# Grouped-query decode attention with a gated FFN on one core: K and V blocks alternate, and eight row blocks of wo go between the last two V blocks

## The chip, the cores and the metric

The kernel runs on one core of one Trainium2 chip. The metric is the device time of one execution in microseconds (us); lower is better. Three runs of the kernel before took 357.87 (median), 356.19 and 358.83 us.

## The reference

One token is decoded. The result is a gated mix of an attention branch with a cached K and V of 32768 positions and of a small SwiGLU branch. All inputs are bf16.

```python
# x 1x1x512, wq 512x4096, k_cache and v_cache 1x8x32768x128, wo 4096x512
# w_gate, w_up 512x1792, w_down 1792x512, gate_w 512
g = sigmoid((x * gate_w).sum(-1, keepdims=True))
q = (x @ wq) as 32 heads of 128                      # 4 query heads per K/V head
p = softmax(q . k * 128 ** -0.5)                     # over 32768 positions
a = (p . v, as one row of 4096) @ wo
b = (silu(x @ w_gate) * (x @ w_up)) @ w_down
out = g * a + (1 - g) * b
```

K and V are 134.2 of the 148.1 MB that are read. With one query position, each of these bytes is used once.

## The kernel before

**Blocks and pages.** There are G = 8 groups (K/V heads). K and V of a group are each cut into NB = 2 blocks of 16384 positions, 4.19 MB or 32 KB per partition. SBUF holds five pages of that size. K's two blocks use pages 0 and 2 (`PG_K`), V's two blocks pages 1 and 3 (`PG_V`). Page 3 holds w_gate and w_up first (`PG_F`), and page 4 (`PG_X`) holds wq first and wo at the end.

**Loads.** All of these loads are issued by SyncE (SP), strictly in the order of its program, onto one queue. Each issue may first wait. `load_k(g, b)` (L278) waits until TensorE has transposed all of block b of K of the group before (`sem_fill`), since that frees the page. `load_v(g, b)` (L283) waits until TensorE has finished with block b of V of the group before (`sem_v_free`); for group 0 the second V block waits until w_gate and w_up are used (`sem_pe_h`). The order is: wq, w_gate, w_up, both K blocks of group 0, the first V block of group 0, both K blocks of group 1, the second V block of group 0; then, for each further group g, both K blocks of g and both V blocks of g - 1; then both V blocks of group 7, w_down (`wd`), and wo in five pieces.

**TensorE.** A loop (L508) makes nine passes, i = 0, 16, ..., 128. In pass g it does `emit_k` (L403) for both blocks of group g, and then `emit_v` (L429) for both V blocks of group g - 1. The first pass skips the V part, the last one skips the K part and ends with `emit_end`. The parts are skipped with `pe.If` on the loop's register.

- `emit_k(i, b)` waits for the page and works in 8 units. For each unit, `emit_fill` makes 8 transposes (L382, two bf16 positions at a time as fp32) into PSUM, VectorE copies the result to SBUF (`ktT`, L663), and `emit_scores` (L394) makes 16 matmuls with q; the scores run two units behind the transposes. VectorE then takes the maximum over the block (L668).
- The maximum over all positions of a group needs both of its K blocks. GpSimd reduces it over the partitions (`gmax`, L266), and ScalarE writes the exponentials of both blocks into `ET` (L541); it waits until the V block of the group before has used that half of `ET` (`sem_v_free`).
- `emit_v(i, b)` waits for the V page and for the exponentials and makes 32 matmuls of 512 columns into `ps_o` (L438). Ahead of the first block, `emit_reduce` (L416) gathers what the group before has left in `acc` (8 matmul records, L420). ScalarE copies `ps_o` to `acc` (L553) when both V blocks are done.

**The end.** `emit_end` (L471) sums the exponentials, reduces the last group, multiplies `wd` (14 matmuls of 512 columns, `emit_wide`, L450, rotating over four strips of PSUM partitions into `ps_w`), brings the attention output into the order of wo's rows (`O2`), and goes through wo's 32 row blocks. The first piece (20 blocks) uses `emit_wide`; VectorE copies `ps_w` to `part` (L699). Each later block uses `emit_rows` (4 matmuls of 128 columns, L461), and `part` is added with the same helper. Then the row is cast (L701) and stored.

Of the kernel before, what the change touches and what calls it, by code (L numbers as in the profile page):

```python
# [13 lines left out]
def bass_gated_mix__gqa_block_cached__swiglu_ffn__decode_kernel(  # L14
# [14 lines left out]
    G = A_k_cache.shape[1]  # L29
# [13 lines left out]
    NB = S // BLK  # L43
# [10 lines left out]
    STEP = 16  # L54
    WOJ = H * DH // 128
    SCALE = float(DH) ** -0.5
    assert UPG == STEP and UPP % NKT == 0 and UPP % NST == 0
    assert KC * H * DH <= PAGE and 2 * KC * F <= PAGE and WOJ * NOUT <= PAGE
    WO_CUTS = [0, 20, 26, 29, 31, 32]
    OC = NOUT // 128  # L60

    RQ = 4
# [1 line left out]
    NSTRIP = 4  # L64
# [8 lines left out]
    with ExitStack() as es:  # L73
        def S_(name):
            return es.enter_context(nc.semaphore(name))
# [3 lines left out]
        sem_f = S_("s_f")  # L79
        sem_wo = [S_(f"s_wo{i}") for i in range(len(WO_CUTS) - 1)]  # L80
        sem_ld_x = S_("s_ld_x")
# [13 lines left out]
        sem_pe_q = S_("s_pe_q")  # L95
# [31 lines left out]
        def T(name, shape, dt):  # L127
            return es.enter_context(nc.sbuf_tensor(name, shape, dt))
# [44 lines left out]
        O2 = T("O2", [128, WOJ], BF16)  # L173
# [27 lines left out]
        wo_v = page[:, PG_X, 0 : WOJ * NOUT].rearrange("p (j n) -> p j n", j=WOJ)  # L201

        with nc.Block("main") as block:
# [66 lines left out]
            @block.sync  # L270
            def _(sp):
                def cache(which, g, b, p, sem):
                    sp.dma_start(  # L273
                        page[:, p, :].rearrange("p (r d) -> p r d", d=DH),
                        which[0, g, b * BLK : (b + 1) * BLK, :].rearrange("(p r) d -> p r d", r=R),
                    ).then_inc(sem, 16)

                def load_k(g, b):  # L278
                    if g:
                        sp.wait_ge(sem_fill, UPG * (g - 1) + UPP * (b + 1))  # L280
                    cache(A_k_cache, g, b, PG_K[b], sem_page[PG_K[b]])

                def load_v(g, b):  # L283
                    if g:
                        sp.wait_ge(sem_v_free, NB * (g - 1) + b + 1)
                    elif PG_V[b] == PG_F:
                        sp.wait_ge(sem_pe_h, 1)
                    cache(A_v_cache, g, b, PG_V[b], sem_page[PG_V[b]])

                sp.dma_start(wq_v, A_wq.rearrange("(p c) n -> p c n", c=KC)).then_inc(sem_q, 16)  # L290
                for w, src in enumerate((B_w_gate, B_w_up)):
                    sp.dma_start(  # L292
                        wgu[:, w, :, :], src.rearrange("(p c) f -> p c f", c=KC)
                    ).then_inc(sem_f, 16)
                for b in range(NB):
                    load_k(0, b)
                load_v(0, 0)
                for b in range(NB):
                    load_k(1, b)
                load_v(0, 1)  # L300
                for g in range(2, G):
                    for b in range(NB):
                        load_k(g, b)
                    for b in range(NB):
                        load_v(g - 1, b)
                for b in range(NB):
                    load_v(G - 1, b)
                sp.dma_start(  # L308
                    wd[:, :, :], B_w_down.rearrange("(p j) n -> p j n", j=FC)
                ).then_inc(sem_ld_wd, 16)  # L310
                sp.wait_ge(sem_pe_q, 1)
                src = A_wo.rearrange("(p j) n -> p j n", j=WOJ)
                for k, s in enumerate(sem_wo):
                    a, b = WO_CUTS[k], WO_CUTS[k + 1]
                    sp.dma_start(wo_v[:, a:b, :], src[:, a:b, :]).then_inc(s, 16)
                sp.wait_ge(sem_dve_row, 1)
                sp.dma_start(
                    out[0, 0, :].rearrange("(c n) -> c n", c=OC),
                    res_row[0 : 32 * (OC - 1) + 1 : 32, :],
                ).then_inc(sem_out, 16)  # L320
                sp.wait_ge(sem_out, 16)

            @block.tensor
            def _(pe):
                pe.wait_ge(sem_ld_x, 32)
                pe.wait_ge(sem_const, 1)
                for src, base in ((x_row, M_X0), (gw_row, M_X0 + KC)):
                    srcv = src[0:1, :].rearrange("o (p c) -> o c p", c=KC)
                    for c in range(KC):
                        ins = pe.matmul(  # L330
                            ps_m[:, base + c : base + c + 1],
                            srcv[:, c, :],
                            ones_bf[0:1, 0:1],
                            start=True,
                            stop=True,
                        )
# [4 lines left out]
                for h in range(H):  # L341
                    for c in range(KC):
                        ins = pe.matmul(  # L343
                            ps_m[:, M_Q0 + h : M_Q0 + h + 1],
                            wq_v[:, c, h * DH : (h + 1) * DH],
                            xT[:, c : c + 1],
                            start=(c == 0),
                            stop=(c == KC - 1),
                        )
# [3 lines left out]
                for e in range(2):  # L353
                    ins = pe.matmul(
                        ps_o[:, e * H : (e + 1) * H],
                        perm[:, e, :],
                        qT[:, :],
                        start=True,
                        stop=True,
                    )  # L360
# [3 lines left out]
                for w, base in enumerate((M_G0, M_U0)):  # L364
                    for j in range(FC):
                        for c in range(KC):
                            ins = pe.matmul(  # L367
                                ps_m[:, base + j : base + j + 1],
                                wgu[:, w, c, :].rearrange("d (p j) -> d j p", j=FC)[:, j, :],
                                xT[:, c : c + 1],  # L370
                                start=(c == 0),
                                stop=(c == KC - 1),
                            )
# [74 lines left out]
                def emit_wide(w, vec, j, first, last):  # L448
                    c = j % NSTRIP
                    return pe.matmul(  # L450
                        ps_w[32 * c : 32 * c + 1, :],
                        vec[:, j : j + 1],
                        w[:, j, :],
                        start=first,
                        stop=last,
                        skip_group_check=True,
                    )
# [13 lines left out]
                def emit_end():  # L471
                    pe.wait_ge(sem_dve_esum2, 1)
                    pe.matmul(  # L473
                        ps_e[:, 0:H],
                        ones_f[:, :],
                        esum2[:, :, :].rearrange("p g h -> p (g h)"),
                        start=True,
                        stop=True,
                    ).then_inc(sem_pe_S, 1)
                    emit_reduce((G + 1) * STEP)  # L480
                    pe.wait_ge(sem_dve_tT, 1)
                    pe.wait_ge(sem_ld_wd, 16)
                    pe.wait_ge(sem_psw, 1)
                    for j in range(FC):
                        emit_wide(wd, tT, j, j < NSTRIP, False)
                    pe.wait_ge(sem_dve_oT2, 1)
                    pe.wait_ge(sem_dve_pm, 1)
                    pe.matmul(
                        ps_m[:, M_O0 : M_O0 + WOJ], pmat[:, :], O2a[:, :], start=True, stop=True
                    ).then_inc(sem_pe_O2, 1)  # L490
                    pe.wait_ge(sem_dve_O2, 1)
                    for k, s in enumerate(sem_wo):
                        pe.wait_ge(s, 16)
                        for j in range(WO_CUTS[k], WO_CUTS[k + 1]):
                            if k == 0:
                                ins = emit_wide(wo_v, O2, j, False, j >= WO_CUTS[1] - NSTRIP)
                            else:
                                ins = emit_rows(
                                    O2[:, j : j + 1], wo_v[:, j, :], j == WO_CUTS[1], j == WOJ - 1
                                )  # L500
                        if k == 0:
                            ins.then_inc(sem_pe_w, 1)
                        if k == 1:
                            pe.wait_ge(sem_dve_w, 1)
                            emit_rows(sel4[:, 0:1], part[:, :], False, False)
                    ins.then_inc(sem_pe_sum, 1)

                with pe.Fori(0, (G + 1) * STEP, STEP) as i:  # L508
                    with pe.If(i < G * STEP):
                        for b in range(NB):  # L510
                            emit_k(i, b)
                    with pe.If(i > 0):
                        for b in range(NB):
                            emit_v(i, b)
                    with pe.If(i > (G - 1) * STEP):
                        emit_end()
# [213 lines left out]
```

## Time and profile before

| | |
|---|---|
| median of three runs | 357.87 us |
| profiled execution: time, span | 358.76 us, 357.0 us |
| granted TensorE clock, mean | 0.871 |
| read from HBM, mean rate over the span | 148.11 MB, 415 GB/s |
| DMA queue of the loads, share of 16 engines | 97.1% |
| TensorE matmuls, weight loads, VectorE, ScalarE busy | 71%, 61%, 50%, 9% |
| chain that ended last: DMA, TensorE, VectorE | 61%, 35%, 3% |
| a K load, a V load, issue to landing (median) | 26.2 us, 30.9 us |
| five wo loads, issue to landing | 28.9, 30.3, 30.7, 31.0, 30.8 us |

The span is the profiled execution as the trace has it. The chain that ended last is followed back from the last instruction, at each step to what released it; its shares tell which kind of work the end waited for, where busy shares don't.

### The profile page before, as it was taken

Reading aid. Unit: us, or ns where it says so; the run is one execution under the profiler, and the core shown is the slowest. Engines: PE = TensorE matmul, PEld = TensorE weight load, DVE = VectorE, ACT = ScalarE, POOL = GpSimd, SP = SyncE. Lnnn points to the kernel's source line nnn. Section 1 sums busy time; section 2 is a strip of 40 time slices with the busy share of each in tenths; the row PEclk is TensorE's granted clock in tenths of the full one; section 3 lists DMA queues with packets and bytes.
Section 4 is the critical chain, followed back from the end, with each engine's and each line's share of the span. In section 5 each row is a group of like instructions: output and inputs, shape, how many; then the busy total and the mean of one; then the engine's idle time right before and its main releaser. Section 6 shows DMA issues by size and latency. Waiting matters only on the chain.

```text
span 357.0 us, 8699 instructions
## 1 busy us (share of the span) xinstructions
PE 252.9 (71%) x3999; PEld 218.6 (61%) x3999; DVE 177.8 (50%) x203; ACT 33.5 (9%) x148; POOL 5.8 (2%) x24
## 2 busy tenths in 40 slices
PE   0346984989989639881989369993987288991364
PEld 0346983989789339860988169952986078941132
DVE  1211984688489118850688028920985048910011
ACT  1000003100400210022000400022001200021000
POOL 0200000000000000000000000000000000000000
PEclk9999998799999859998899959966999869966666
DMA  8999999999999999999999999999999999949995
GB/s 334 406 422 457 417 417 443 424 422 437 430 422 448 422 427 444 422 426 448 419 430 452 411 437 444 411 441 441 411 441 441 408 444 437 415 158 415 416 442 229
DMA packets 5925, 148.24 MB, mean 415 GB/s; under 512 B 666, under 2 KB 796, under 8 KB 1180
## 3 DMA queue, kind: packets, MB, share of 16 engines
q1 hardware_dynamic: 5912, 148.12, 97.1%
q8 instruction: 6, 0.10, 0.1%
q14 instruction: 3, 0.02, 0.0%
q10 hardware_dynamic: 4, 0.00, 0.0%
HBM read 148.11 MB, written 0.00 MB: 415 GB/s over the span
## 4 chain that ended last, share of the span: by engine, by line
DMA 61%; PE 35%; DVE 3%; SPq 1%; issue 1%
DMA page<-in_A_k_cache_dram 52%; PE pst L382 24%; DMA page<-in_A_wo_dram 8%; PE ps_sc L394 6%; DVE ktT L663 3%; PE ps_o L438 3%; PE ps_m L420 1%; PE pst L450 1%; PE pst L461 0%; SPq L292 0%; DVE part L699 0%; SPq L308 0%; SPq L290 0%; SPq L273 0%; DVE res_row L701 0%
## 5 line engine op out<-in xcount | busy, mean ns | idle before, releaser
L663 DVE COPY ktT<-pst 128x2048 bf16<-128x2048 bf16 x128 | 155.6, 1224 | 102.9 <-PE pst L382 95.5
L382 PE MATMUL pst<-ident_f,page 128*128 128x128 f32 x1024 | 147.7, 297 | 48.9 <-DMA page<-in_A_k_cache_dram 44.8
L382 PEld LDWEIGHTS pst<-ident_f,page 128*128 128x128 f32 x1024 | 124.4, 153 | 54.8 <-DMA page<-in_A_k_cache_dram 47.9
L394 PE MATMUL ps_sc<-qcur,ktT 128*128 128x8 bf16 x2048 | 67.7, 166 | 8.6 <-DVE ktT L663 8.6
L394 PEld LDWEIGHTS ps_sc<-qcur,ktT 128*128 128x128 bf16 x2048 | 66.6, 97 | 11.2 <-DVE ktT L663 10.0
L438 PE MATMUL ps_o<-page,ET 128*16 128x512 bf16 x512 | 39.7, 471 | 18.8 <-DMA page<-in_A_v_cache_dram 17.3
L438 PEld LDWEIGHTS ps_o<-page,ET 128*16 128x16 bf16 x512 | 13.7, 104 | 40.2 <-issue 24.8
L541 ACT ACTIVATE ET<-ps_sc,nbias 128x128 bf16<-128x128 f32 x64 | 25.3, 546 | 24.2 <-PE ps_o L438 24.1
L532 ACT ACTIVATE nbias<-gmax 128x4 f32<-128x4 f32 x8 | 1.6, 206 | 237.3 <-POOL gmax L266 237.3
L541 ACT ACTIVATION_READ_ACCUMULATOR ET<-ps_sc,nbias 128x1 f32 x64 | 17.5, 274 | 0.0
L668 DVE TENSOR_REDUCE pmaxf<-ps_sc 128x4 f32<-128x512 f32 x16 | 11.1, 692 | 10.4 <-PE ps_sc L394 10.4
L420 PE MATMUL ps_m<-sel,acc 128*128 128x4 f32 x72 | 10.9, 275 | 2.6 <-ACT acc L553 2.6
L420 PEld LDWEIGHTS ps_m<-sel,acc 128*128 128x128 f32 x72 | 10.3, 220 | 3.2 <-ACT acc L553 3.2
L685 DVE RECIPROCAL rS<-pst 128x32 f32<-128x32 f32 x1 | 0.4, 358 | 19.5 <-PE pst L473 19.5
L367 PE MATMUL ps_m<-xT,page 128*128 128x1 bf16 x112 | 6.9, 198 | 4.1 <-DMA page<-in_B_w_up_dram 4.1
L367 PEld LDWEIGHTS ps_m<-xT,page 128*128 128x128 bf16 x112 | 6.8, 160 | 4.2 <-DMA page<-in_B_w_up_dram 4.2
L266 POOL PARTITION_ALL_REDUCE gmax<-pmax x8 | 3.0, 372 | 284.8 <-DVE pmax L670 284.8
L343 PE MATMUL ps_m<-xT,page 128*128 128x1 bf16 x128 | 3.6, 165 | 5.1 <-DMA page<-in_A_wq_dram 5.1
L553 ACT ACTIVATE acc<-ps_o 128x512 f32<-128x512 f32 x8 | 5.0, 629 | 21.0 <-PE ps_o L438 21.0
L343 PEld LDWEIGHTS ps_m<-xT,page 128*128 128x128 bf16 x128 | 3.5, 104 | 5.2 <-issue 5.2
L330 PE MATMUL ps_m<-ones_bf,x_row 1*128 1x1 bf16 x4 | 0.3, 172 | 8.1 <-DMA gw_row<-in_gate_w_dram 8.1
L330 PEld LDWEIGHTS ps_m<-ones_bf,x_row 1*128 1x128 bf16 x4 | 0.2, 114 | 8.1 <-DMA gw_row<-in_gate_w_dram 8.1
(68 smaller groups left out, 27.1 us busy)
## 6 DMA issues: line engine op xcount, KB each, us to landing
page<-in_A_k_cache_dram SPq DMA_DIRECT2D x16, 4096.0 KB, 26.2
page<-in_A_v_cache_dram SPq DMA_DIRECT2D x16, 4096.0 KB, 30.9
page<-in_A_wq_dram SPq DMA_DIRECT2D x1, 4096.0 KB, 12.8
page<-in_A_wo_dram SPq DMA_DIRECT2D x1, 2560.0 KB, 28.9
page<-in_B_w_gate_dram SPq DMA_DIRECT2D x1, 1792.0 KB, 16.6
page<-in_B_w_up_dram SPq DMA_DIRECT2D x1, 1792.0 KB, 21.1
wd<-in_B_w_down_dram SPq DMA_DIRECT2D x1, 1792.0 KB, 23.2
page<-in_A_wo_dram SPq DMA_DIRECT2D x1, 768.0 KB, 30.3
```

The lines of the kernel that those rows point to most:

```text
L266: pool.partition_all_reduce(gmax[:, g, :], pmax[:, g, :], 128, ReduceOp.max).then_inc(sem_gmax, 1)
L343: ins = pe.matmul(ps_m[:, M_Q0 + h : M_Q0 + h + 1], wq_v[:, c, h * DH : (h + 1) * DH], xT[:, c : c + 1], start=(c == 0), stop=(c == KC - 1),)
L367: ins = pe.matmul(ps_m[:, base + j : base + j + 1], wgu[:, w, c, :].rearrange("d (p j) -> d j p", j=FC)[:, j, :], xT[:, c : c + 1], start= ...
L382: ins = pe.transpose(pst[u % NST][:, k * 128 : (k + 1) * 128], kv[:, n * 128 : (n + 1) * 128], ident_f[:, :],)
L394: ins = pe.matmul(ps_sc[b][:, col : col + 2 * HPG], kt[:, k, e, :], qcur[:, e, :], start=(e == 0), stop=(e == 1),)
L420: ins = pe.matmul(ps_m[:, M_P0 : M_P0 + HPG], acc[:, q, :], sel4[:, q * HPG : (q + 1) * HPG], start=(q == 0), stop=(q == RQ - 1),)
L438: ins = pe.matmul(ps_o[32 * c : 32 * c + RQ * HPG, :], ET[:, n : n + RQ, :].rearrange("p n h -> p (n h)"), view[:, k * RQ : (k + 1) * RQ, ...
L450: return pe.matmul(ps_w[32 * c : 32 * c + 1, :], vec[:, j : j + 1], w[:, j, :], start=first, stop=last, skip_group_check=True,)
L541: act.activation(ET[:, b * R : (b + 1) * R, h], sc[:, h, :], ACT.Exp, bias=nbias[:, g, h : h + 1], scale=SCALE, accum_out=esum[:, g, b, h ...
L553: act.activation(acc[:, :, :].rearrange("p q d -> p (q d)"), ps_o[:, :], ACT.Copy).then_inc(sem_acc, STEP)
L663: dve.tensor_copy(ktT[:, u % NKT, :], pst[u % NST][:, :].bitcast(BF16)).then_inc(sem_cp, 1)
L668: dve.tensor_reduce(pmaxf[:, f, :], sc, AX.X, ALU.max).then_inc(sem_pmax, 1)
```

## The change

SP alternates K and V blocks, in the order in which TensorE's new loop takes them: block 0 of K, block 0 of the V of the group before, block 1 of K, block 1 of that V. Each of the four parts of a pass has its own `If`. The first wo piece, now eight row blocks, is loaded between the two V blocks of group 7, and `sem_pe_q` (wq is used) is waited for there. The pieces of wo become 8, 10, 8, 4 and 2 row blocks instead of 20, 6, 3, 2 and 1, and the first two of them (18 blocks) use `emit_wide`.

```diff
-    WO_CUTS = [0, 20, 26, 29, 31, 32]
+    WO_CUTS = [0, 8, 18, 26, 30, 32]
+    WIDE = WO_CUTS[2]
...
                 load_v(0, 0)
-                for b in range(NB):
-                    load_k(1, b)
+                load_k(1, 0)
                 load_v(0, 1)
+                load_k(1, 1)
                 for g in range(2, G):
                     for b in range(NB):
                         load_k(g, b)
-                    for b in range(NB):
                         load_v(g - 1, b)
-                for b in range(NB):
-                    load_v(G - 1, b)
+
+                def load_wo(k):
+                    a, b = WO_CUTS[k], WO_CUTS[k + 1]
+                    src = A_wo.rearrange("(p j) n -> p j n", j=WOJ)
+                    sp.dma_start(wo_v[:, a:b, :], src[:, a:b, :]).then_inc(sem_wo[k], 16)
+
+                load_v(G - 1, 0)
+                sp.wait_ge(sem_pe_q, 1)
+                load_wo(0)
+                load_v(G - 1, 1)
                 sp.dma_start(
                     wd[:, :, :], B_w_down.rearrange("(p j) n -> p j n", j=FC)
                 ).then_inc(sem_ld_wd, 16)
-                sp.wait_ge(sem_pe_q, 1)
-                src = A_wo.rearrange("(p j) n -> p j n", j=WOJ)
-                for k, s in enumerate(sem_wo):
-                    a, b = WO_CUTS[k], WO_CUTS[k + 1]
-                    sp.dma_start(wo_v[:, a:b, :], src[:, a:b, :]).then_inc(s, 16)
+                for k in range(1, len(sem_wo)):
+                    load_wo(k)
...
-                            if k == 0:
-                                ins = emit_wide(wo_v, O2, j, False, j >= WO_CUTS[1] - NSTRIP)
+                            if j < WIDE:
+                                ins = emit_wide(wo_v, O2, j, False, j >= WIDE - NSTRIP)
                             else:
                                 ins = emit_rows(
-                                    O2[:, j : j + 1], wo_v[:, j, :], j == WO_CUTS[1], j == WOJ - 1
+                                    O2[:, j : j + 1], wo_v[:, j, :], j == WIDE, j == WOJ - 1
                                 )
-                        if k == 0:
+                        if k == 1:
                             ins.then_inc(sem_pe_w, 1)
-                        if k == 1:
+                        if k == 2:
                             pe.wait_ge(sem_dve_w, 1)
                             emit_rows(sel4[:, 0:1], part[:, :], False, False)
...
-                    with pe.If(i < G * STEP):
-                        for b in range(NB):
+                    for b in range(NB):
+                        with pe.If(i < G * STEP):
                             emit_k(i, b)
-                    with pe.If(i > 0):
-                        for b in range(NB):
+                        with pe.If(i > 0):
                             emit_v(i, b)
```

## The prediction

> **What bounds the kernel now.** First I read the slices of the page: what the DMA engines moved, and how busy they were.
>
> ```profile
> DMA  8999999999999999999999999999999999949995
> GB/s 334 406 422 457 417 417 443 424 422 437 430 422 448 422 427 444 422 426 448 419 430 452 411 437 444 411 441 441 411 441 441 408 444 437 415 158 415 416 442 229
> ```
>
> The transfers are the bound almost everywhere (9 in nearly all slices), and there is one hole: slice 36 of 40, about 312 to 321 us, with 158 GB/s. Next, the chain that ended last, in order of time:
>
> ```profile
> 102.65 28.11 DMA page<-in_A_k_cache_dram
> ...
> 142.50 27.16 DMA page<-in_A_k_cache_dram
> ...
> 180.97 27.58 DMA page<-in_A_k_cache_dram
> ...
> 320.69 0.33 SPq L273
> ```
>
> It is a loop: the first K block of a group lands, TensorE transposes it, its page is reloaded, and the load lands some 27 to 28 us later. That long landing is queueing: three other 4.19 MB blocks stand ahead. The first transposes of groups 3 and 7 start at 130.81 and 287.33, so a group takes 39.13 us; its four blocks are 16.78 MB, so 428.8 GB/s and **9.78 us a block**. Any order with a full queue runs at this pace. The chain then leaves the loop and passes through the issue of the last V block at 320.69. So, last, the hole by the microsecond (columns: stretch, its length, busy time of PE, PEld, DVE, ACT, POOL, then TensorE's granted clock, DMA share, GB/s) and the timeline around it:
>
> ```profile
> 312.00:313.00 1.00, 0.66 (x19) 0.67 (x19) 0.35 (x2) 0.00 (x0) 0.00 (x0) 0.99 0.84 360
> 313.00:314.00 1.00, 1.00 (x7) 1.00 (x7) 0.79 (x2) 0.00 (x0) 0.09 (x1) 0.50 0.08 33
> ...
> 317.00:318.00 1.00, 1.00 (x16) 0.29 (x8) 0.00 (x0) 0.00 (x0) 0.00 (x0) 0.50 0.00 0
> 318.00:319.00 1.00, 1.00 (x16) 0.30 (x12) 0.00 (x0) 0.95 (x5) 0.00 (x0) 0.50 0.74 197
> ```
>
> ```profile
> 312.75 1.65 PE L420 MATMUL ps_m<-sel,acc 128*128 128x4 f32 x8
> ...
> 314.33 6.31 PE L438 MATMUL ps_o<-page,ET 128*16 128x512 bf16 x64
> ...
> 317.97 3.06 SPq L273 DMA_DIRECT2D page<-in_A_v_cache_dram  x2
> ...
> 330.40 3.39 PE L438 MATMUL ps_o<-page,ET 128*16 128x512 bf16 x32 [6.02 <-DMA page<-in_A_v_cache_dram]
> ...
> 340.12 3.59 PE L438 MATMUL ps_o<-page,ET 128*16 128x512 bf16 x32 [6.33 <-DMA page<-in_A_v_cache_dram]
> ```
>
> The last two V loads can be issued only when TensorE is done with the V blocks of group 6. That work stands behind both K blocks of group 7, which end at 312.9. The queue has run dry at 313.1 but for two late packets (quarter-microsecond windows put them at 313.5 and 314.75), and SP issues at 317.97 and 320.7. This is the only hole: 133.7 MB stand ahead of it, and at 428.8 GB/s from 1.5 us on they end at 313.3.
>
> **The change, part by part.**
>
> (a) *Load order K, V, K, V.* Bytes, number of issues and pages stay. What changes is when each load's wait is met, against when its turn in the queue comes. A K block alone takes 13.26 us on TensorE:
>
> ```profile
> 63.13 4.81 PE L382 MATMUL pst<-ident_f,page 128*128 128x128 f32 x24 [5.38 <-DMA page<-in_A_k_cache_dram]
> ...
> 75.83 0.56 PE L394 MATMUL ps_sc<-qcur,ktT 128*128 128x8 bf16 x16 [0.54 <-DVE ktT L663]
> ```
>
> Its last transpose is done 11.4 us after landing (63.13 to 74.54, where the next load goes out). With a first K block landing at 0, the others land at 9.8, 19.6 and 29.3, the next group at 39.1. The next K load goes out at 11.4 and its turn comes after the load landing at 29.3: 18 us to spare. The V block runs behind K from 13.3 to 17.9 at most (reduction 1.0 to 1.65, 32 matmuls 1.8 to 3.5); its turn comes at 39.1, 21 us to spare. The second half is the same. SP issues strictly in order, and this order is TensorE's own, so no wait holds back a load that could go. At the start, V of group 0, second block, is now issued behind the wait for the first K page (44.12) instead of the second (56.2): earlier, onto a page free since 29.7, with the queue filled to about 49. K of group 1, second block, moves one turn back (9.8 us) and is issued at 55.9 as before. Cost 0.
>
> (b) *TensorE order.* The four blocks of a pass cost 2 x 13.26 + 1.0 + 3.6 = 31.1 us warm. They no longer pair K with K, where two took 25.0 (63.13 to 88.16), so 1.5 us is added under a cover of 39.1 - 31.1 = 8 us of waiting for K loads. Cost 0; without cover, 1.5 us a pass. A second, shorter idle gap per pass may keep the granted clock at 0.50 longer: in the cold pass from 287.33 the first 24 transposes took 5.34 instead of 4.65, the whole block 13.8 (to 301.12), V 3.5 a block, the reduction 1.65. All cold: 2 x 13.8 + 1.65 + 7.0 = 36.3 us, still below 39.1. The Trainium skill speaks against such an order: "TensorE: Matmul & The Clock Gate", section "Why this matters for your kernels", wants no gaps over about 3 us between bursts of matmuls. By it the all-cold sum would hold in every pass; by the rows (1.00 in most of a K block) the first. The end is the same by either.
>
> (c) *Four skips instead of two.* They are taken in pass 0 (both V parts) and pass 8 (both K parts), and each stands before a wait for a load or a 5 us wait. Nearest row: 0.43 us of "issue" at the jump back to the loop's top at 92.55; at the If passed at 88.0, nothing. From 0 to 0.43 each; no gain is possible. I take 0, since all are covered. "Runtime: NRT & Kernel Launch", section "Instruction fetch mechanics", warns that a taken branch out of the fetched window stalls on a fetch of its target. It gives no time; a stall would fall into the same waits.
>
> (d) *Last V blocks.* Bytes ahead of the first K of group 7 are unchanged, so it lands at 287.3 again. Then, by bytes: V6 first 297.1, K7 second 306.9, V6 second 316.6, V7 first 326.4, eight rows of wo (1.05 MB, 2.45 us) 328.9, V7 second 338.7, wd (1.84 MB) 342.9, the other wo rows (3.15 MB) 350.3. V7 first is issued by 306.4, when V6 first is done (287.3 + 13.8 + 1.65 + 3.5 + 0.1); the queue then reaches to 313.1, so the hole at 313 goes. V7 second waits for V6 second, which TensorE reaches after K7 second: 306.9 + 13.3 (cold 13.8) + 1.8 (cold 3.5) = 322.0 to 324.2. Behind V7 second on SP wait wd and all other wo loads. The queue's data ends earlier than its landings: at 313.1 + 9.78 + 2.45 = 325.3. That leaves 1.1 to 3.3 us, and issue to data takes about 0.5 (317.97 to 318.4). Without the wo rows there it would be -1.3 to +0.9, so a new hole: they are the cover.
>
> (e) *The gain.* From landings: the last wo load is issued at 323.5 and takes 30.8, so it lands at 354.3; new 350.3, **4.0 us**. From the data: the queue is empty from 313.0 to 318.4, **5.4 us**. The difference is stragglers: single engines run up to 1.7 us behind in a long queue (the packet at 314.75), and the pause lets them catch up. I take 4.7, midway.
>
> (f) *Tail.* O2 is ready 6.7 us after the last V landing (340.12 to 346.82): new 345.4. Then 8 + 10 wide matmuls of 0.115 (20 took 2.30; the second piece lands at 346.0) end at 347.5, the part copy (0.70) at 348.2, and 32 row matmuls of 0.035 from 348.5 (their landing) at 349.6; partial sums 0.4, 16 and 8 more row matmuls 0.8: 350.9. That is 0.6 behind the last landing; before it is 354.62 - 354.3 = 0.3. Cost 0.3; bounds 0 (rows at 0.025, as at full clock) and 0.6.
>
> **Sum:** -4.7 + 0.3 = -4.4 us; 357.0 - 4.4 = 352.6 of span. The profiled execution took 358.76, 0.89 above the median of the runs shown (357.87), so it becomes 354.4 and the median **353.5**. Bounds: -5.4 + 0 gives 352.5, -4.0 + 0.6 gives 354.5; with 0.6 for the median of few runs (they spread from 356.19 to 358.83), 351.9 to 355.1.
>
> **Rivals.**
> *The hole moves* to the last V block, if K7 second and V6 second end 2 us later than worked out. For: only 1.1 us is left when the clock is 0.50, as it was there before. Against: wo covers 2.45. Price 2 us: 355.5.
> *No gain shows*: the pause only moved stragglers, and the last landing lags the data (313.1 + 33.6 = 346.7) by 7.6 us, not by the 3.6 in the sum. For: the first block after the pause took 12.4 us to land. Against: from there on 9.7 a block. About 357.9.
> *TensorE becomes the bound* (slower): stalls at the Ifs, fall-through ones too. It decides once a pass exceeds 39.1, so from (39.1 - 36.3) / 4 = 0.7 us per If, everything cold. At 1 us each a pass takes 40.3, 1.2 over, in 8 passes 9.6 us more, less 4.4: 363.1. Against: nothing at 88.0, 0.43 at 92.55.
>
> **Chances.** Forecast 0.70, hole moved 0.16, no gain 0.05, TensorE bound 0.09. A measurement of this kernel can tell about 1% from no change, so faster is below 354.3. Of the forecast 0.58 lies there and 0.12 above; of the moved hole 0.02 and 0.14; no gain is "same". Faster 0.60, same 0.31, slower 0.09. The range runs from 351.9 up to 356.0, which takes in the moved hole; it leaves out no gain, TensorE bound and some 0.05 of the tails.
>
> **What would show it.** Right: no slice near 312 to 321 below 400 GB/s; the last V issued at 322 to 324.5; last V matmuls from about 338.7; span near 352.6; idle time of TensorE before K blocks split over both K blocks, with K to landing still 27 to 28 us. Wrong: a gap in the data between the last two V blocks, K blocks that begin without a wait for their load, or "issue" idle of over 0.7 us at the Ifs.

## The result, and the profile after

| | kernel before | changed kernel |
|---|---|---|
| median, 14 runs each | 355.89 us | 354.31 us |
| lowest and highest | 355.08, 358.83 us | 353.79, 354.86 us |
| profiled execution: time, span | 358.76, 357.0 us | 353.97, 352.2 us |
| mean rate over the span | 415 GB/s | 421 GB/s |

The ratio of the times is 0.9945, 95% interval 0.9924 to 0.9966: faster by some 0.55%, clear of the noise, but less than the 1% that the prediction counted as faster. That is inside the range on record (351.9 to 356.0) and on the forecast's side, but it is a third of the 4.4 us that the sum gave. The profiled execution agrees far better (span 352.2, predicted 352.6). So the question of the experiments is why one comparison gives 4.8 us and the other 1.6.

The slices of the page after:

```profile
DMA  8999999999999999999999999999999999999994
GB/s 328 411 443 422 437 437 423 419 424 447 435 421 424 447 436 417 424 443 443 417 424 435 447 421 424 435 443 424 424 435 443 424 421 435 443 424 412 426 425 170
```

The hole is gone: no slice but the first and the last is below 411 GB/s. The timeline around the last V blocks (start, duration, engine, line, tiles; lines 387 and 443 are 382 and 438 of before):

```profile
286.54 4.54 PE L387 MATMUL pst<-ident_f,page 128*128 128x128 f32 x24 [5.44 <-DMA page<-in_A_k_cache_dram]
...
300.75 3.34 PE L443 MATMUL ps_o<-page,ET 128*16 128x512 bf16 x32
...
304.52 0.43 SPq L310 DMA_DIRECT2D page<-in_A_wo_dram  x1
...
305.93 1.97 PE L387 MATMUL pst<-ident_f,page 128*128 128x128 f32 x16 [1.84 <-DMA page<-in_A_k_cache_dram]
...
317.81 1.90 PE L443 MATMUL ps_o<-page,ET 128*16 128x512 bf16 x32
...
319.76 0.33 SPq L274 DMA_DIRECT2D page<-in_A_v_cache_dram  x1
...
325.47 3.59 PE L443 MATMUL ps_o<-page,ET 128*16 128x512 bf16 x32 [1.35 <-DMA page<-in_A_v_cache_dram]
...
337.67 3.59 PE L443 MATMUL ps_o<-page,ET 128*16 128x512 bf16 x32 [8.61 <-DMA page<-in_A_v_cache_dram]
```

The first V block of group 6 is done at 304.1, 1.8 us ahead of the second K block of group 7. It runs at the slow clock here too (3.34 us), and that costs nothing: SP issues the next V load and the first wo piece at once, while the queue still holds some 9 us of data (an estimate: by the prediction's bytes it reaches to 313.1). The last V load goes out at 319.76, before its turn. From landing to landing the last two V blocks are 12.2 us apart, which is a V block (9.78) and a quarter of wo (2.45): no pause.

### The profile page after: what moved, and what is told of

It reads as the page before. It is cut to its first block, busy times and chain, and to the rows that moved or that the text cites. A ratio compares the mean times of both kernels' runs of the same rounds, so it can differ in the third digit from the quotient of the medians.

```text
span 352.2 us, 8737 instructions
## 1 busy us (share of the span) xinstructions
PE 266.7 (76%) x4005; PEld 227.3 (65%) x4005; DVE 177.5 (50%) x203; ACT 32.3 (9%) x148; POOL 5.8 (2%) x24
## 4 chain that ended last, share of the span: by engine, by line
DMA 62%; PE 33%; DVE 3%; SPq 1%; issue 0%
DMA page<-in_A_k_cache_dram 55%; PE pst L387 24%; DMA page<-in_A_wo_dram 7%; PE ps_sc L399 6%; DVE ktT L667 3%; PE ps_o L443 2%; PE pst L466 1%; PE ps_m L425 0%; SPq L293 0%; SPq L310 0%; SPq L316 0%; SPq L291 0%; SPq L274 0%; DVE res_row L705 0%
## 5 line engine op out<-in xcount | busy, mean ns | idle before, releaser
L387 PE MATMUL pst<-ident_f,page 128*128 128x128 f32 x1024 | 156.1, 309 | 40.7 <-DMA page<-in_A_k_cache_dram 38.9
L387 PEld LDWEIGHTS pst<-ident_f,page 128*128 128x128 f32 x1024 | 132.5, 160 | 52.2 <-DMA page<-in_A_k_cache_dram 46.9
L443 PE MATMUL ps_o<-page,ET 128*16 128x512 bf16 x512 | 44.3, 507 | 10.0 <-DMA page<-in_A_v_cache_dram 10.0
L545 ACT ACTIVATE ET<-ps_sc,nbias 128x128 bf16<-128x128 f32 x64 | 24.1, 553 | 0.7
(68 smaller groups left out, 27.6 us busy)
## 6 DMA issues: line engine op xcount, KB each, us to landing
page<-in_A_k_cache_dram SPq DMA_DIRECT2D x16, 4096.0 KB, 27.6
```

What stands on the lines that cost most here:

```text
L387: ins = pe.transpose(pst[u % NST][:, k * 128 : (k + 1) * 128], kv[:, n * 128 : (n + 1) * 128], ident_f[:, :],)
L443: ins = pe.matmul(ps_o[32 * c : 32 * c + RQ * HPG, :], ET[:, n : n + RQ, :].rearrange("p n h -> p (n h)"), view[:, k * RQ : (k + 1) * RQ, ...
L545: act.activation(ET[:, b * R : (b + 1) * R, h], sc[:, h, :], ACT.Exp, bias=nbias[:, g, h : h + 1], scale=SCALE, accum_out=esum[:, g, b, h ...
```

## The experiments

Theory: the change is worth the pause in the queue ahead of the last two V loads and nothing else; how long the pause is in a run of before depends on when TensorE gets through V of group 6. Rivals: the K, V, K, V order streams better by itself; the pause only moved stragglers; runs of before differ in their streaming rate.

**The kernel before, four more profiles.** No edit.

> The kernel before, unchanged, for a second profile. Pause theory: the time is either near 355.5 or near 358 us, and the trace tells which by TensorE's clock after the second K block of group 7: at clock 1.00 the reduction takes 1.0 and the first V block of group 6 1.8 us, the last but one V load goes out 2.4 us earlier against its K block, and the pause in the data is 3 us; at 0.50 it is 5.4 us as in the first profile, and the time near 358. Rate theory (the long runs just stream more slowly): the pause is 5.4 us in either, and the group's period differs, 38.8 against 39.1 us.

> The kernel before, unchanged, third profile. Pause theory with the clock as what sets its size: a time near 358.2 goes with V of group 6 at 3.4 to 3.6 us a block (clock 0.50) and a pause near 5 us, one near 355.5 with 1.8 to 1.9 us a block and a pause near 2 us. If the clock is not what splits the runs, the two are mixed.

> The same, fourth profile: same pairs of time, V duration and pause.

> The same, fifth profile: same pairs of time, V duration and pause.

Measured: 356.02, 358.11, 358.18 and 358.64 us. In the first, and then in the third of them, the landing of group 7's first K block, the end of its second one, the V loads, and the landing of its first V block:

```profile
287.16 4.78 PE L382 MATMUL pst<-ident_f,page 128*128 128x128 f32 x24 [8.71 <-DMA page<-in_A_k_cache_dram]
...
312.02 1.03 PE L420 MATMUL ps_m<-sel,acc 128*128 128x4 f32 x8
...
312.99 1.90 PE L438 MATMUL ps_o<-page,ET 128*16 128x512 bf16 x32
...
314.94 3.73 SPq L273 DMA_DIRECT2D page<-in_A_v_cache_dram  x2
...
327.35 3.59 PE L438 MATMUL ps_o<-page,ET 128*16 128x512 bf16 x32 [5.81 <-DMA page<-in_A_v_cache_dram]
```

```profile
287.33 4.38 PE L382 MATMUL pst<-ident_f,page 128*128 128x128 f32 x24 [6.58 <-DMA page<-in_A_k_cache_dram]
...
312.82 1.03 PE L420 MATMUL ps_m<-sel,acc 128*128 128x4 f32 x8
313.78 5.32 PE L438 MATMUL ps_o<-page,ET 128*16 128x512 bf16 x64
...
317.24 2.23 SPq L273 DMA_DIRECT2D page<-in_A_v_cache_dram  x2
...
329.53 3.59 PE L438 MATMUL ps_o<-page,ET 128*16 128x512 bf16 x32 [7.20 <-DMA page<-in_A_v_cache_dram]
```

And the data by the microsecond, of the same two (the third number from the end is TensorE's granted clock, the last one GB/s):

```profile
313.00:314.00 1.00, 1.00 (x21) 0.50 (x24) 0.26 (x2) 0.20 (x1) 0.37 (x1) 1.00 0.31 131
314.00:315.00 1.00, 0.89 (x20) 0.20 (x8) 0.00 (x0) 0.00 (x0) 0.00 (x0) 1.00 0.08 33
315.00:316.00 1.00, 0.00 (x0) 0.00 (x0) 0.00 (x0) 0.97 (x6) 0.00 (x0) 1.00 0.71 197
```

```profile
315.00:316.00 1.00, 1.00 (x16) 0.31 (x8) 0.00 (x0) 0.00 (x0) 0.00 (x0) 0.50 0.00 0
316.00:317.00 1.00, 1.00 (x16) 0.33 (x12) 0.00 (x0) 0.00 (x0) 0.00 (x0) 0.50 0.00 0
317.00:318.00 1.00, 1.00 (x20) 0.44 (x16) 0.00 (x0) 0.67 (x4) 0.00 (x0) 0.79 0.00 0
```

At clock 1.00 the first V block takes 1.90 us, the V load goes out at 314.94, and only some 2 us pass without data. With the clock at 0.50 for most of the V block, the load goes out between 317.2 and 318.0 (four profiles, the first of them the one in the prediction), with 4 to 5 us of hardly any data, and the times are 358.1 to 358.8. The group's period doesn't differ: 38.89 us from 130.64 to 169.53 in the shortest run, 38.88 from 130.81 to 169.69 in the third. So the rate rival falls, and the times of before go in two bunches with the time at which TensorE gets through that V block. Of the 2.3 to 3.0 us by which the load goes out later in the long runs, 1.5 to 1.7 are the V block itself, at the lower clock; the rest is that the block starts later (313.8 to 314.3 instead of 312.99). In the 23 runs beside the next experiments, 14 lie from 355.15 to 356.68 and 9 from 357.62 to 358.67, none between. The long ones have been profiled four times, the short one once. Why the clock is lower in some runs and not in others, no run here shows.

What a pause costs can be read from landings. Four blocks land between group 7's first K block and its first V block, 39.1 us of a full queue. The short run took 40.2 (287.16 to 327.35), the long ones 42.2 to 43.1 (in the prediction's profile 287.33 to 330.40), the changed kernel 38.9 (286.54 to 325.47). So the pause delayed the landings by 1.1 us in the short run and by 3.1 to 4.0 in the long ones, each time some 1 to 1.7 us less than the time without data.

**w_down as the filler.** The order of groups stays K, K, V, V; only w_down is moved.

```diff
+                sp.dma_start(wd[:, :, :], ...).then_inc(sem_ld_wd, 16)
                 for b in range(NB):
                     load_v(G - 1, b)
-                sp.dma_start(wd[:, :, :], ...).then_inc(sem_ld_wd, 16)
```

> The kernel before with one move: w_down is loaded ahead of the last two V blocks instead of behind them; K, K, V, V order and wo pieces as before. Pause theory: w_down's 1.84 MB (4.3 us) fill the pause, of which 0 to 1.1 us stay; wo is now all that follows the last V block (9.8 us), and O2, ready 6.7 us after that landing, puts about 1 us on the tail; the gain is 2 us when the pause was 3 and 3.4 when it was 5.4, so about 353.9 to 354.5, as the change. Alternation theory (the order K, V, K, V streams better by itself): no gain, about 355.9, and a slower tail.

> The kernel with w_down ahead of the last V blocks, second profile, to see what spreads its times from 354.0 to 357.0 us. Either the pause is not covered when the clock is 0.50 (a gap in the data near 317, last V landing late, time near 356.5), or the data come on time and the tail is on TensorE: 20 wide matmuls of wo in 2.3 instead of 1.25 us and rows at 0.035 instead of 0.025, so the end 1.5 to 2.5 us behind the last landing instead of 0.3.

Measured: 355.31 us median of 12 runs (354.02 to 356.95), ratio 0.9969 (0.994 to 0.9998); the second profile took 354.03. The first profile:

```profile
280.63 0.43 SPq L306 DMA_DIRECT2D wd<-in_B_w_down_dram  x1
317.10 2.06 SPq L273 DMA_DIRECT2D page<-in_A_v_cache_dram  x2
```

The clock was 0.50 over the V block and the V load as late as in the long runs (317.10), yet nothing was lost: the first V block of group 7 landed 43.3 us after its first K block (286.92 to 330.19), which is four blocks and w_down (39.1 and 4.3), and the time was 354.24. That is the changed kernel's time without its alternation, so in these runs the alternation shows no gain of its own. The median is 1.0 us above the changed kernel's, though, and above what was expected: of the 1.6 us that the change gains in the median, w_down as the filler gains 0.7. Both profiles caught short runs, with the tail at clock 1.00 only 0.3 us behind the last landing; that the longer ones have a slow tail on TensorE, where more of wo now follows the last V block, is argued and not shown, and so a use of the new order or of the new wo pieces in those runs isn't excluded.

**The loads alone.** The kernel before with SP's order alternated in all groups, TensorE's not.

```diff
-                for b in range(NB):
-                    load_k(1, b)
+                load_k(1, 0)
                 load_v(0, 1)
+                load_k(1, 1)
...
                     for b in range(NB):
                         load_k(g, b)
-                    for b in range(NB):
                         load_v(g - 1, b)
```

> The kernel before with only the load order of groups 0 to 7 alternated (K, V, K, V); TensorE still takes K, K, V, V, and w_down and wo come last as before. Pause theory: V of group 6 is taken only after the second K block of group 7, which now lands one turn later (about 306.9) and ends at 320.1; the last but one V load goes out at 323 (clock 1.00) to 325.5 (0.50), with the queue empty since 313.1: a pause of 10 to 13 us, 362 to 366 us. Alternation theory: loads alternate as in the changed kernel, so about 354.3 to 356.

Measured: 384.01 us, ratio 1.0732 (1.0665 to 1.0799). The sign was right, the size missed by 20 us:

```profile
GB/s 329 419 441 433 433 423 424 431 431 133 219 438 438 438 380 439 438 431 339 438 438 438 404 414 424 434 434 345 438 434 438 278 434 438 284 0 421 428 422 235
```

```profile
301.65 0.33 SPq L273 DMA_DIRECT2D page<-in_A_v_cache_dram  x1
302.02 0.43 SPq L273 DMA_DIRECT2D page<-in_A_k_cache_dram  x1
```

The expected hole at the end is there: the slices with 284 and 0 lack 576 of 860 GB/s in 19.2 us, 12.8 us of transfers. But the expectation looked at the end alone. A K load now stands behind a V load whose page TensorE frees only after both K blocks, so the second K load of every group goes out right behind that V load, however early its own page was free. SP waited 212.5 us in all for V matmuls instead of 86.8. The queue runs dry in most groups; the start alone (133 and 219) lacks 11 us.

**TensorE alone.** The kernel before with the four skippable parts, loads unchanged.

```diff
-                    with pe.If(i < G * STEP):
-                        for b in range(NB):
+                    for b in range(NB):
+                        with pe.If(i < G * STEP):
                             emit_k(i, b)
-                    with pe.If(i > 0):
-                        for b in range(NB):
+                        with pe.If(i > 0):
                             emit_v(i, b)
```

> The kernel before with only TensorE's order alternated (four skippable parts); loads stay K, K, V, V and the end as before. Each V block is then needed before the second K block, but lands behind it. Pause theory: K of group 7 lands at 287.3 and 297.1, V of group 6 at 306.9 and 316.6; TensorE does the second K block only after V at 306.9, to 322 (clock 1.00) or 324, the second V to 324 or 327.7; the queue runs dry at 322.9 ahead of the last V load: a pause of 1.5 to 5 us, 354.5 to 358.5. In passes 1 to 7 the K load of the second block goes out about 11 us later (issued when the queue still holds 6 us), so no pause there; if SP's order makes one as in the run with the loads alone, 8 times 3 us, so 380.

Measured: 357.31 us (356.13 to 358.69), ratio 1.0018 (0.9988 to 1.0049): the same as before within what can be told, and within the expected 354.5 to 358.5. The profile has the pause at the new place:

```profile
322.99 1.90 PE L438 MATMUL ps_o<-page,ET 128*16 128x512 bf16 x32
...
325.31 0.43 SPq L308 DMA_DIRECT2D wd<-in_B_w_down_dram  x1
```

The second V block of group 6 runs at 322.99, the last V load goes out just ahead of w_down, and the microsecond from 324 moves 98 GB/s. The last V block lands 50.1 us after group 7's first K block, where five blocks of a full queue take 48.9: 1.2 us lost, about what the short run of before lost. Each half of the reordering by itself gains nothing or loses; together they match.

**Without the wo rows between the last V blocks.** The changed kernel with its first wo piece behind w_down.

```diff
                 load_v(G - 1, 0)
+                load_v(G - 1, 1)
                 sp.wait_ge(sem_pe_q, 1)
-                load_wo(0)
-                load_v(G - 1, 1)
...
-                for k in range(1, len(sem_wo)):
+                for k in range(len(sem_wo)):
                     load_wo(k)
```

> The changed kernel with the eight wo row blocks loaded behind w_down again, so that nothing stands between the last two V blocks. My prediction's own step: the last V load goes out 1.3 us too early to 0.9 us too late, so a pause of up to 1.4 us and 354.3 to 355.7. Trace of the changed kernel (last V load issued at 319.76, queue's data without wo to 322.8): 3 us to spare, no pause, the same time as the changed kernel within 0.3 us.

Measured: 354.32 us (354.05 to 354.88), against 354.31 with them. The last V load goes out just ahead of w_down (321.28), with the queue's data lasting to about 322.8. The rows between the V blocks bring nothing that 12 runs show.

**Extra work behind the second K block**, in the kernel before, the changed one and the one without wo between the V blocks.

```diff
+                def emit_extra():
+                    for k in range(96):
+                        c = k % NSTRIP
+                        pe.matmul(
+                            pst[1][32 * c : 32 * c + RQ * HPG, 0:256],
+                            ident[:, 0 : RQ * HPG],
...
                             emit_k(i, b)
+                        emit_extra()
```

The cut shows the kernel before; in the other two the call stands behind `emit_k` under `if b == 1:`.

> The kernel before with 96 extra matmuls (256 columns each, of constants, written to a PSUM bank that nothing reads until it is rewritten) behind the second K block of each group; nothing is left out. By the V matmuls' rows (32 of 512 columns in 1.8 us at clock 1.00, 3.5 at 0.50) they take 2.7 or 5.4 us. Pause theory: they stand ahead of V of group 6, so the pause grows by all of it: 358.2 to 363, from 355.5. If the time before the last V loads did not set the end (stragglers, rate): under 0.5 us.

> The changed kernel with the same 96 extra matmuls behind the second K block of each group. Pause theory: the last V load goes out at 322.5 (clock 1.00) or 325.2 (0.50, and up to 327 when V is slow too), against data that keep the queue busy to 325.3 with the eight wo rows in between, less 0.5 from issue to data: no loss at clock 1.00 (354.3), at most 2 us at 0.50. A kernel bound by TensorE would lose 8 x 2.7 us.

> The changed kernel without wo between the last two V blocks, with the same 96 extra matmuls. The queue's data end at 322.8: at clock 1.00 the last V load at 322.5 to 323.7 costs 0.2 to 1.4 us (354.5 to 355.7), at 0.50 2.5 to 4.5 us (357 to 359). If the wo rows between the V blocks did nothing, the same time as with them.

Measured: 362.69 us (361.94 to 364.86), 356.24 (355.3 to 357.37) and 356.62 (355.19 to 358.21); against the kernel before without extra work the ratios are 1.0171 (1.0113 to 1.0229), 0.9997 (0.9967 to 1.0027) and 1.0013 (0.998 to 1.0046). Ahead of the last V loads the kernel before now shows (same columns as above):

```profile
313.00:318.00 5.00, 4.46 (x107) 3.86 (x109) 3.58 (x5) 0.06 (x1) 0.37 (x1) 0.85 0.99 426
318.00:324.00 6.00, 6.00 (x124) 3.94 (x120) 0.16 (x1) 0.28 (x2) 0.00 (x0) 0.84 0.01 5
```

Six microseconds without data, 4 more than at clock 1.00 without the extra work, which took 4.5 us there. By landings, group 7's first V block comes 45.1 us after its first K block, 6.0 more than a full queue takes. In the other two the three microseconds around the last V load move at least 262 GB/s (issued at 325.68) and 328 GB/s (at 323.6); in the changed kernel a microsecond of a full queue can be as low as 229. There the last V block lands 51.1 us (with the wo rows) and 48.7 us (without) after group 7's first K block, where a full queue takes 51.4 and 48.9: nothing is lost. So the same work on TensorE lengthens the pause before and is hidden after, as the theory wants. But all three also lost time that none of the theories had, early in the run (last section): with wo between the V blocks 1.61 MB moved from 80 to 86 us, where 428.8 GB/s would have moved 2.57, so 2.2 us; in the kernel before 0.82 of 2.14 MB from 79 to 84 and 0.69 of 1.72 from 92 to 96, so 5.5 us; without wo between them 1.31 of 2.14 MB from 79 to 84, so 1.9 us. So the totals are no test of the theory, though 362.69 lies inside what was expected: part of each is this early loss. With and without the wo rows the medians are 0.4 us apart in spreads of 2 and 3 us: a use for the rows isn't shown here either.

## Why the prediction was right or wrong, point by point

**What bounds the kernel: right.** One hole in a full queue, made by V pages that come free late. Moving TensorE's and SP's order together removes it, and w_down in the hole does the same.

**The pause, and the time it was subtracted from (steps e and the sum): wrong in size.** The sum took 4.7 us off, from the pause of one profiled execution (5.4 us without data, 4.0 by landings), and then an offset of 0.89 us to the median as if it were a constant. The execution was of the longer bunch, and so were two of the three runs shown. In the shorter bunch, where the median of 14 runs lies, the one profile has a pause of some 2 us, 1.1 by landings. The change takes away whatever pause there is, and its own times spread over 1.07 us where before they spread over 3.75. So the absolute time of a profiled run was met (353.97 for 354.4), and the median was not moved down by 0.89 but stayed at the level of the runs (354.31 for 353.5). Against the long runs the gain is 4.8 us (358.76 to 353.97), predicted 4.4; against the shortest ones 1.3 (355.08 to 353.79). That 4.8 comes so near to 4.4 is in part luck: 4.0 of it is the pause, and 0.8 stands ahead of it, since group 7's first K block landed at 286.54 here and at 287.33 in that profile (286.74 to 287.53 in the other four of before). The prediction had the evidence: it named 1.8 or 3.5 us a V block by the clock in step (a), and 0.50 through the hole in its own fence, but priced it only for the new order.

**Chances.** 0.60 stood on faster by over 1%; what came is 0.55%, inside "same", which had 0.31. The forecast of one number from one profile was too sure of the base; the range held because it was wide enough for the 0.8 us by which the median was off.

**K, V, K, V at no cost (a, b): right**, and only since both halves were changed. Idle time of TensorE before K blocks is 38.9 us in 13 waits instead of 44.8 in 7, and K loads take 27.6 us to landing, as foreseen. TensorE does run colder: a transpose takes 309 ns instead of 297 in the mean, the mean granted clock is 0.849 instead of 0.871 in the profiled runs (medians of the runs 0.853 and 0.871), and none of it reaches the end. The rule on gaps between bursts, weighed in step (b), doesn't decide between the orders: the waits for K loads were 7 of 6.4 us in the mean before and are 13 of 3.0 now, and the clock fell to 0.50 within busy stretches too (the prediction's row from 313.00). What makes it colder, no run here shows.

**Four skips (c): right in the cost, not in the bounds.** The skip between the first two K blocks shows 0.29 us of "issue" in the profile of the changed kernel (bounds 0 to 0.43). In the other traces with four skips it shows 0.24 to 1.15, and 0.90 in the kernel without the wo rows, which at 354.07 us lost nothing by it. The nearest row, 0.43 at a later jump, was no bound for the first pass (last section).

**The last V load (d): wrong in a term.** It went out at 319.76, predicted 322.0 to 324.2. Of the 2.2 us to the nearer bound, 1.0 is that the second K block landed at 305.93 and not at 306.9, and 1.3 that I took 13.26 us for a K block at full clock from one whose first 24 transposes ran at 0.58; the one here took 11.95 (305.93 to 317.88). With 3 us to spare the wo rows cover nothing, where the step called them the cover.

**Tail (f): right.** The last piece of wo is waited for at 349.4, TensorE ends at 349.82 (0.4 behind; predicted 0.6).

**Rivals.** No moved hole, no bound on TensorE. "No gain, only stragglers" falls with the span of 352.2 and with w_down as the filler. What holds of it is that each pause cost the landings some 1 to 1.7 us less than its time without data.

## What to carry to other kernels

A pause in a full transfer queue is worth what it delays the landings by, here some 1 to 1.7 us less than the time without data. Read it in several executions before it is priced: one that ends on another engine's pace and clock differed by a factor of three between runs here, and the median of a few runs may sit in either bunch. Buffers come free in the order in which the consumer takes them, and a queue issued in order must follow that order: change both or neither. A filler that waits for nothing, put ahead of the late load, gained as much as the new order in its short runs, and less in the median.

## What the runs showed of the hardware that was not expected

TensorE sat idle with no wait that the profile shows in the three kernels with extra matmuls, in the first pass. Of the kernel before with them:

```profile
63.27 0.39 PE L451 MATMUL pst<-perm,ident 128*16 128x256 bf16 x6 [2.72 <-issue]
...
70.28 4.70 PE L382 MATMUL pst<-ident_f,page 128*128 128x128 f32 x24 [6.62 <-issue]
```

The first gap, 2.72 us, lies inside a straight run of 96 matmuls with no semaphore between them; the second, 6.62 us, at the jump back to the top of the loop. The changed kernel with them has 6.29 us at the same jump, the one without the wo rows 5.18. These delays opened the early holes in the data: the K load that waits for these transposes goes out at 81.64 instead of 74.54 us in the kernel before.

The gap is not peculiar to the extra work. Three of the five profiles of the kernel before have 4.85, 5.80 and 7.10 us of "issue" at this jump, the kernel with the loads alone 6.40, the changed kernel without the wo rows 3.62. Most of that is the wait for the K load, which "issue" hides: the transposes start there at 63.20 to 65.49 us, where the profiles of the kernel before that name the load as what ended the wait have 62.75 and 63.13. With the extra work they start at 68.92 to 70.28. No matmul of the fourteen traces shows such a gap after 71 us.

The Trainium skill, "Runtime: NRT & Kernel Launch", section "Instruction fetch mechanics", says that a taken branch out of the fetched window stalls on a fetch. The traces fit it: in all eight traces with such a gap at this jump, TensorE goes on 2.2 to 2.3 us after a 16 KB packet of the instruction queue has landed (68.02 and then 70.28 in the rows above; 66.73 and 69.00 in the changed kernel with extra work; 61.00 and 63.20 in the short run of before). These packets come some 6 to 7 us apart at that time, the kernels with extra work need one more of them (seven instead of six from 18 us on), and none comes after 75 us, so only the first pass pays. The page calls the fetch of straight code mostly hidden; the first gap, inside straight code, ends 1.3 us after such a packet (62.02), and if it is a fetch, this one was not hidden. Whose instructions the packets carry and why they are so far apart, no run here shows.
